# A hand-written order list of 1364 words, dealt anew behind its first 60 words

## The chip, the core and the metric

The kernel runs on one core of one Trainium2 chip. The metric is the device time of one execution in microseconds (us), lower is better. The engines that matter here are TensorE (PE, with its weight loads as a row of their own, PEld), VectorE (DVE), ScalarE (ACT), GpSimd (POOL) and SyncE (SP), which in this kernel does nothing but issue transfers.

## The reference

Two branches read the same layer-normalised input `xn` (2048 rows of 512) and are added to the input:

```python
x = A_x                                   # 1 x 2048 x 512, bf16
xn = _layernorm(x, axis=-1)
return x + _A_ref(xn, A_wq, A_wk, A_wv, A_wo, A_beta) + _B_ref(xn, B_w1, B_w2)
```

Branch B is `silu(xn @ w1) @ w2` with 1792 hidden columns. Branch A is attention with 32 heads of 16 in four segments of 512 rows. In each segment every head does causal softmax attention inside the segment (`a_dot`), and besides reads a memory of the earlier segments (`a_mem = phi(q) M / (phi(q) z)`, with `phi(t) = t + 1` above zero and `exp(t)` below); the two are mixed by a gate, `g * a_mem + (1 - g) * a_dot`, and the result goes through `wo`. After each segment `M` and `z` grow by the segment's keys and values.

## The kernel before, in words

**Tiles and banks.** Everything is kept in SBUF: the transposed `xnT`, all weights, and per segment the tiles `qT`, `kT`, `hT` (hidden activations) and `oT` (attention output). PSUM has eight banks. Four belong to `psS`, the scores of one step; the other four are a pool (`pb`) from which every other sum takes one bank: `ps` (projections, hidden sums, the memory product), `psV` (weights times values), `psM` and `psO` (an output row block). A sum that needs a bank waits until an earlier holder was copied out by DVE or ACT.

**The order list.** The program is not written as loops. A string `ORDER` holds 1364 words, and the last loop of the kernel calls one small function a word, in the order of the list. An engine runs its own instructions in exactly that order, so the list sets each engine's queue, and the words of different engines only stand beside each other. The words that the text needs, with segment `s` and column group or row block as numbers:

- `S0` to `S71`: a score step (`scores`, L716): TensorE multiplies queries by keys in four row strips into `psS`, ACT takes the exponential of all 2048 columns (L722, into one of six buffers `Pb`), POOL masks (L736). A line break in the list stands ahead of each `S`.
- `E0`, `O0` and so on: weights times values (`weigh`, L783), even and odd heads, in column strips; `Ev`, `Ov`, `Ea`, `Oa` copy the bank out (DVE or ACT) and move the softmax sums to the tile `zraw` by two small transfers (L805); `Om` merges odd heads into `oraw`.
- `h`, `ha`, `hv`: hidden sums, tanh on ACT (L483), and the product on DVE (L488). `k`, `q`, `v` with `kv`, `qv`, `vv`: projections and their copies.
- `r`, `w` (last segment: `R`, `W`): reciprocals of the sums (L536, L551) and the gate (L541, L557); `z`, `d` spread them over partitions by two transfers each (L568, tile `spr`), `zv`, `dv` multiply (L580, L590); `n`, `nv` are the memory product and its addition into `oT` (L599).
- `o`, `oc`, `od`: one output product (512, 256 or 128 columns) of a row block; each block needs 18 of the 512-column kind, 14 from `hT` and 4 from `oT`. `xl` loads the residual rows (L605), `st` adds them and stores the block (L612 on DVE, then the store's issue at L617). `oh` and `sh`: the last block is summed and stored in two halves (256 columns each, L659 and the store's issue at L663).

These last words, above all the `o` family, are filler: they may stand nearly anywhere behind their inputs, and they fill TensorE between the score steps.

**One piece or four strips.** A 128-column product is issued either as one matmul (L336) or as four matmuls of 32 columns side by side (L338). Which it is follows from the list: a product behind an `S` takes the form of the next `S`, `E`, `O` or like word, so that TensorE changes its tile form as seldom as can be. 

Of the kernel before, what the change touches and what calls it, by code (L numbers as in the profile page):

```python
# [19 lines left out]
S3 v0.2.0 v0.2.1 Nv4 h0.1.2 h0.1.3 v0.2.2 XD7 v0.2.3 K0.1 hv0.0 vv0.2 k0.2.1 k0.2.2 k0.2.3 kv0.2 XD4 ha0.1  # L20
S1 lw1.1 v0.3.0 tanh v0.3.1 fa0.1 omask h0.2.0 h0.2.1 lw0.12 xs8 q0.3.0 fp0.0 v0.3.2 lw0.13 lw0.5 v0.3.3 h0.2.2 q0.3.1
S4 q0.3.2 q0.3.3 Nv6 hv0.1 vv0.3 lw1.3 qv0.3 lw0.1 XD6 v1.3.0 v1.3.1 v1.3.2 xs11 h0.4.0 h0.2.3 ha0.2 v1.3.3 vv1.3 h0.3.0 XD5 hv0.2
S5 h0.4.1 K0.2 h0.3.1 h0.4.2 kind h0.3.2 h0.3.3 ha0.3 fv0.1 h0.4.3 E0
S6 v1.0.0 v1.0.1 v1.0.2 v1.0.3 Ev0 fp0.3 ha0.4 hv0.3 vv1.0 v1.2.0 v1.2.1 v1.2.2 xs10 v1.2.3 q1.0.0
S7 vv1.2 xs9 xg8.4 q1.0.1 q1.0.2 h0.6.0 h0.6.1 O0 hv0.4 Ov0 fa0.3 h0.6.2 lw0.10 h0.6.3
S8 q1.0.3 qv1.0 E1 Ev1 fv0.3 q1.1.0 q1.1.1 ha0.6 h0.8.0 h0.8.1 q1.1.2
S9 v1.1.0 hv0.6 Nv10 q1.1.3 Om0 v1.1.1 Nv11 qv1.1 v1.1.2 v1.1.3 k1.2.0 gp1.1 vv1.1 k1.2.1 t0.3 fa0.2 k1.2.2 k1.2.3
S12 fv0.0 kv1.2 K0.3 h0.8.2 h0.5.0 h0.5.1 h0.5.2 h0.5.3 XD11 ha0.5 fp0.2 Nv8 XD10 XD8 h0.7.0 h0.7.1 h0.7.2 hv0.5 h0.8.3 ha0.8 hv0.8
S10 q1.2.0 q1.2.1 q1.2.2 q1.2.3 qv1.2 h0.7.3 k1.0.0 lw0.9 t0.1 ha0.7 Nv9 lw1.2 k1.0.1 k1.0.2 XD9 k1.0.3 h0.10.0 kv1.0
S13 h0.10.1 O1 hv0.7 Ov1 q1.3.0 q1.3.1 q1.3.2 k1.3.0 q1.3.3 qv1.3 ga1.1  # L30
S11 fv0.2 h0.10.2 fp1.0 k1.3.1 t0.2 t0.0 k1.3.2 k1.3.3 xs15 kv1.3 h1.1.0 h1.1.1 h0.10.3 k1.1.0 lw0.0 lw0.11 ha0.10 h1.1.2 h1.1.3 ha1.1 hv0.10
S15 k1.1.1 hv1.1 h0.9.0 h0.9.1 h0.9.2 E2 K1.0 h0.9.3 ha0.9 h1.2.0 xs14 gv1.1 hv0.9 h1.2.1
S14 h1.2.2 h1.2.3 Ev2 k1.1.2 k1.1.3 kv1.1 xs12 ha1.2 hv1.2 O2 k2.2.0 lw0.4
S17 h1.10.0 h1.10.1 k2.2.1 kv2.2 lw1.0 h1.10.2 h1.10.3 ha1.10 gate h0.11.0 h0.11.1 h0.11.2 Ov2 lw0.8 lw0.6
S16 h0.12.0 h0.11.3 ha0.11 h0.12.1 h0.12.2 hv1.10 E3 Om2 Ev3 lw0.2 lw0.7 xl0.0 K1.1 hv0.11 k2.1.0 h0.12.3 ha0.12 K1.2
S20 k2.1.1 h0.13.0 h0.13.1 h0.13.2 kv2.1 hv0.12 O3 fp1.2 Ov3 m0.2 mv0.2 h0.13.3 fa1.0 Om1
S18 q2.1.0 q2.1.1 v2.2.0 m0.0 qv2.1 v2.2.1 lw0.3 ha0.13 fv1.0 K1.3
S19 mv0.0 k2.0.0 k2.0.1 hv0.13 v2.1.0 v2.1.1 kv2.0 fa1.2 h1.11.0
S22 vv2.2 sv0 r0.1 q2.3.0 vv2.1 h1.11.1 h1.11.2 xs13 xg12.4 o0.2.12 h1.11.3 q2.3.1 ha1.11 hv1.11 o0.2.7
S24 qv2.3 o0.2.4 od0.2.11.2 h1.8.0 h1.8.1 h1.8.2 h1.8.3 o0.2.13 h1.0.0 oc0.2.6.0 o0.2.1 od0.2.11.1 ha1.8 r0.2 r0.0  # L40
S25 E4 o0.2.2 h1.0.1 r0.3 w0 o0.2.8 z0.1 h1.0.2 h1.0.3 xl0.2 ha1.0 z0.2 hv1.8 Ev4 od0.2.11.0 h1.7.0 Nv15
S21 hv1.0 K2.1 h1.4.0 h1.7.1 h1.4.1 fv1.2 h1.7.2 h1.7.3 ha1.7 Nv12 XD12 hv1.7 q2.0.0 q2.0.1 XD15
S23 o0.2.3 qv2.0 h1.4.2 h1.4.3 ha1.4 o0.2.0 od0.2.11.3 fp1.1 z0.0 zv0.1 O4 z0.3 Ov4 k2.3.0
S26 zv0.2 fp1.3 k2.3.1 h1.9.0 h1.9.1 h1.9.2 h1.9.3 hv1.4 ha1.9 o0.0.8 K2.0 kv2.3 hv1.9 o0.0.5 o0.0.15
S31 E5 o0.0.4 bmask o0.0.2 od0.0.1.1 oc0.0.3.0 oc0.0.7.1 h1.13.0 Ev5 o0.0.10 fa1.3 h1.13.1
S28 Om3 O5 o0.0.6 Ov5 o0.0.13 Nv13 od0.0.1.0 o0.0.9 h1.13.2 h1.13.3 ha1.13 hv1.13 h1.3.0
S27 oc0.0.7.0 fv1.3 h1.3.1 oc0.0.3.1 h1.3.2 h1.3.3 xl0.3 od0.0.1.2 oc0.2.6.1 zv0.0 h1.12.0 ha1.3 h1.12.1 h1.12.2 hv1.3 XD13 gp1.2 t1.3 h1.12.3 ha1.12 hv1.12 Om5 oc0.2.10.1
# [5 lines left out]
S34 mw0.0 fv2.1 o0.3.7 h1.6.0 o0.3.10 h1.6.1 o0.3.8 od0.3.2.2 od0.3.2.0 Om4 h1.6.2 h1.6.3 oc0.1.2.1 o0.3.11 ha1.6 hv1.6 gp1.3
S40 mw0.2 ga1.3 K2.3 o0.1.1 o0.3.4 O7 Ov7 gv1.3 q3.1.0 q3.1.1 xl0.1 qv3.1 oc0.3.3.0
S42 k3.1.0 o0.1.10 o0.3.13 k3.1.1 kv3.1 oc0.3.1.0 od0.3.2.3 oc0.1.2.0 o0.3.5 m1.2 mv1.2
S36 o0.1.13 o0.1.4 ga2.2 st0.3 od0.1.8.2 s1 sv1 gp2.2 v2.3.0 o0.1.5 K2.2 xl1.1 o1.2.12 r1.0 o0.1.0 m1.0
S37 fp2.0 v2.3.1 o0.1.12 Om6 mv1.0 vv2.3 o0.1.6 o1.2.10 Om7 q3.3.0 fa2.0 q3.3.1
S38 r1.1 qv3.3 h2.8.0 h2.8.1 v3.3.0 t2.1 ha2.8 v3.3.1 r1.3 r1.2 w1 o1.2.8 z1.3
S39 st0.1 hv2.8 od1.2.0.0 od1.2.0.2 vv3.3 z1.1 q3.2.0 q3.2.1 E8 Ev8 v3.0.0 d1.3
S41 qv3.2 v3.0.1 h2.11.0 o1.2.1 d1.2 h2.11.1 k3.0.0 ha2.11 zv1.3  # L60
S49 vv3.0 h1.5.0 h1.5.1 fv2.0 t2.0 h1.5.2 h1.5.3 ha1.5 hv2.11 o1.2.3 gv2.2 k3.0.1 kv3.0 z1.2 E9 hv1.5
S44 fp2.2 k3.2.0 ga2.1 k3.2.1 o1.2.13 xl1.2 v3.2.0 v3.2.1 Ev9 kv3.2 dv1.3
S43 vv3.2 zv1.1 h2.7.0 n1.3 nv1.3 gp2.1 h2.7.1 ha2.7 zv1.2 q3.0.0 q3.0.1
S48 qv3.0 d1.1 d1.0 O8 Ov8 o1.2.6 dv1.2 h2.5.0 h2.5.1 ha2.5 hv2.7 o1.2.4 oc1.2.11.1
S45 oc1.2.2.1 z1.0 K3.2 O9 hv2.5 h2.1.0 Ov9 dv1.0 h2.1.1 dv1.1 ha2.1 h2.12.0
# [869 lines left out]
```

## Time and profile before

| | |
|---|---|
| time, median of 3 runs | 221.25 us (220.82, 221.25, 221.46) |
| the profiled execution's own time | 221.0 us |
| span of that execution, first to last instruction | 219.2 us |
| TensorE busy | 211.5 us (96%) |
| ACT busy | 184.2 us (84%) |
| DVE busy | 180.2 us (82%) |
| POOL busy | 126.7 us (58%) |
| granted TensorE clock | 0.999 |

The times of the profile are counted from the start of the span. Between the span and the execution's own time lie 1.8 us outside the program's instructions. A busy TensorE says only that a matmul was in the pipe; whether it waits is read from its waits and from the stretch in which they fall.

### The profile page before, as it was taken

Reading aid. Unit: us, or ns where it says so; the run is one execution under the profiler, and the core shown is the slowest. Engines: PE = TensorE matmul, PEld = TensorE weight load, DVE = VectorE, ACT = ScalarE, POOL = GpSimd, SP = SyncE. Lnnn points to the kernel's source line nnn. Section 1 sums busy time; section 2 is a strip of 40 time slices with the busy share of each in tenths; the row PEclk is TensorE's granted clock in tenths of the full one; section 3 lists DMA queues with packets and bytes.
Section 4 is the critical chain, followed back from the end, with each engine's and each line's share of the span. In section 5 each row is a group of like instructions: output and inputs, shape, how many; then the busy total and the mean of one; then the engine's idle time right before and its main releaser. Section 6 shows DMA issues by size and latency. Waiting matters only on the chain.

```text
span 219.2 us, 9430 instructions
## 1 busy us (share of the span) xinstructions
PE 211.5 (96%) x4058; PEld 116.5 (53%) x4084; DVE 180.2 (82%) x367; ACT 184.2 (84%) x175; POOL 126.7 (58%) x189
## 2 busy tenths in 40 slices
...
GB/s 199 361 372 126 169 28 52 121 87 114 125 28 13 91 74 73 51 99 7 98 52 82 90 63 15 24 11 98 74 54 89 88 52 82 65 4 88 110 52 99
DMA packets 33530, 19.62 MB, mean 90 GB/s; under 512 B 14928, under 2 KB 33488, under 8 KB 33488
## 3 DMA queue, kind: packets, MB, share of 16 engines
...
q8 instruction: 32, 0.52, 1.0%
...
## 4 chain that ended last, share of the span: by engine, by line
PE 85%; ACT 10%; DVE 2%; issue 1%
PE ps L336 19%; PE psO L338 17%; PE ps L338 16%; PE psS L716 10%; PE psO L336 9%; PE psV L783 8%; ACT Pb L722 6%; PE psS L338 4%; PE psS L856 2%; ACT th L483 1%; ACT ex L414 1%; PE psM L443 1%; ACT L309 1%; ACT xnT L843 0%; ACT Vz L397 0%
## 5 line engine op out<-in xcount | busy, mean ns | idle before, releaser
L722 ACT ACTIVATE Pb<-psS 128x2048 bf16<-128x2048 f32 x72 | 135.2, 1878 | 4.0 <-PE psS L716 2.7
L736 POOL TENSOR_SCALAR_AFFINE_SELECT Pb<-Pb 128x512 bf16<-128x512 bf16 (+1 forms) x72 | 60.0, 834 | 29.8 <-ACT Pb L722 27.0
L488 DVE SCALAR_TENSOR_TENSOR hT<-th,ps 128x512 bf16<-128x512 bf16 x56 | 37.5, 678 | 12.9 <-ACT th L483 12.3
L338 PE MATMUL psO<-w_sb,hT 128*32 128x512 bf16 (+2 forms) x712 | 43.5, 324 | 0.0
L736 POOL TENSOR_SCALAR_AFFINE_SELECT lows<-Pb 64x512 bf16<-64x512 bf16 (+1 forms) x40 | 23.6, 590 | 25.8 <-ACT Pb L722 18.1
L483 ACT ACTIVATE th<-ps 128x512 bf16<-128x512 f32 x56 | 32.6, 596 | 2.2 <-PE ps L338 1.6
L336 PE MATMUL ps<-xnT,w_sb 128*128 128x512 bf16 (+1 forms) x143 | 32.6, 336 | 0.5 <-issue 0.2
L338 PEld LDWEIGHTS <-hT 128*32 128x32 bf16 x880 | 22.2, 97 | 14.5 <-issue 2.3
L338 PE MATMUL ps<-xnT,w_sb 128*32 128x512 bf16 (+1 forms) x516 | 28.8, 337 | 0.0
L716 PE MATMUL psS<-qT,k 32*128 32x64 bf16 (+3 forms) x512 | 23.0, 233 | 0.3
L716 PEld LDWEIGHTS <-k 32*128 32x128 bf16 x512 | 9.7, 92 | 22.6 <-issue 21.8
L783 PE MATMUL psV<-Pb,Vz 128*32 128x448 bf16 (+7 forms) x512 | 21.4, 287 | 0.0
L336 PE MATMUL psO<-w_sb,hT 128*128 128x512 bf16 (+2 forms) x83 | 20.5, 319 | 0.6 <-issue 0.5
L783 PEld LDWEIGHTS <-Vz 128*32 128x32 bf16 x768 | 15.8, 97 | 9.2 <-issue 1.3
L336 PEld LDWEIGHTS <-w_sb 128*128 128x128 bf16 x151 | 13.6, 98 | 11.9 <-issue 2.3
L338 PEld LDWEIGHTS <-w_sb 128*32 128x32 bf16 x516 | 12.9, 97 | 7.4 <-issue 1.1
L382 POOL TENSOR_SCALAR k<-kT,pm_odd 128x512 bf16<-128x512 bf16 x16 | 11.6, 725 | 8.2 <-DVE stats L286 7.1
L716 PE MATMUL psS<-qT,kT 16*128 16x448 bf16 (+3 forms) x256 | 14.7, 269 | 0.0
L612 DVE SCALAR_TENSOR_TENSOR o_out<-psO,x_res 128x512 bf16<-128x512 f32 x14 | 9.6, 688 | 5.9 <-PE psO L338 2.7
L336 PE MATMUL ps<-wv_sb,xnT 128*128 128x512 bf16 x46 | 13.5, 385 | 1.0 <-ACT xnT L843 0.5
L336 PEld LDWEIGHTS <-hT 128*128 128x128 bf16 x88 | 8.2, 98 | 8.8 <-issue 1.3
L820 DVE CAST odd<-psV 128x512 bf16<-128x512 f32 x15 | 10.3, 687 | 3.0 <-PE psV L783 2.8
...
## 6 DMA issues: line engine op xcount, KB each, us to landing
...
```

What stands on the lines that cost most here:

```text
L336: return [nc.tensor.matmul(out, lhsT=lhsT, rhs=rhs, start=start, stop=stop, skip_group_check=True)]
L338: nc.tensor.matmul(out[c : c + 32], lhsT=lhsT[:, c : c + 32], rhs=rhs, start=start, stop=stop, tile_position=(0, c), skip_group_check=True,)
L382: nc.gpsimd.tensor_scalar(out=to, in0=frm, scalar1=keep[:, 0:1], scalar2=1.0, op0=ALU.mult, op1=ALU.mult)
L483: nc.scalar.activation(out=th[:], in_=sts[s]["h", ft][:, :], func=AF.Tanh, scale=0.5)
L488: nc.vector.scalar_tensor_tensor(out=st["hT"][:, ft, :], in0=st.pop(("th", ft))[:], scalar=1.0, in1=st.pop(("h", ft))[:, :], op0=ALU.add, ...
L612: out = nc.vector.scalar_tensor_tensor(out=o_out[:], in0=st.pop(("psO", j)), scalar=0.5, in1=st["x", j][:], op0=ALU.mult, op1=ALU.add)
L716: nc.tensor.matmul(psS[:, g, c : c + q2 - q1], lhsT=keys[rows], rhs=st["qT"][rows, dt, q1:q2], start=True, stop=True, tile_position=(32 * ...
L722: exp = nc.scalar.activation(out=blocks(Pb, b).rearrange("p x g c -> p g x c"), in_=psS[:, :, :].rearrange("p g (x c) -> p g x c", c=block ...
L736: over[id(Pb)].append(nc.gpsimd.affine_select(out=out, in_=in_, compare_op=ALU.is_ge, fill=0.0, base=base, pattern=pattern, channel_multip ...
L783: nc.tensor.matmul(psV[32 * g : 32 * g + 32, q0 : q0 + nq], lhsT=Vzs[s % 2][:, kt, 4 * dt + g, par : par + 2, :].rearrange("p a d -> p (a ...
L820: copy(out=odd[:], in_=sts[s].pop(("psV", 1))[:, :])
L856: nc.tensor.matmul(idle[:, 0:P], lhsT=zraw[:, 0:P], rhs=zraw[:, 0:P], start=True, stop=True)
```

## The change

The list behind its first 60 words is replaced by another list of the same 1364 words. Two of the shorter lines, before and after:

```diff
 ORDER = """
...
-S35 q2.2.0 q2.2.1 o0.1.3 qv2.2 o0.1.16 E7 Ev7 fa2.1 oc0.1.9.0
...
+S35 q2.2.0 q2.2.1 fa2.1 o0.1.14 Om5 o0.3.5 E7 oc0.1.2.0
...
```

The old list ends with the words `st3.1 oh17.1 o3.2.16 o3.0.6 od3.0.2.2 o3.2.17 st3.2 oh17.0 o3.0.17 o3.0.8 o3.0.11 st3.0 oh0.0 oh1.1 oh11.1 oh12.1 oh11.0 oh15.1 oh9.1 oh6.1 oh8.1 sh1 oh10.0 oh7.0 oh16.0 oh6.0 oh13.0 sh0`, the new one with `st3.2 oh17.1 oc3.0.1.1 st3.0 oh16.1 oh14.1 oh7.1 oh15.1 oh2.1 oh14.0 oh9.0 oh10.0 oh12.0 oh16.0 oh6.0 oh13.0 sh1 oh0.0 oh2.0 oh5.0 oh1.0 oh17.0 oh7.0 oh4.0 oh15.0 sh0`.

In the new list `O9` stands between `O8` and `Ov8`, so that two odd sums are open at once. The kernel therefore keeps them under a key with the column group:

```diff
-        psV = st["psV", par] = bank([P, L], F32, "psV")
+        psV = st["psV", par, dt] = bank([P, L], F32, "psV")
...
-        copy(out=oraw[:], in_=sts[s].pop(("psV", 0))[:, :])
+        copy(out=oraw[:], in_=sts[s].pop(("psV", 0, dt))[:, :])
...
-        copy(out=odd[:], in_=sts[s].pop(("psV", 1))[:, :])
+        copy(out=odd[:], in_=sts[s].pop(("psV", 1, dt))[:, :])
```

All words are the same, so every transfer, activation and vector operation is there as often as before. TensorE issues 4033 matmuls instead of 4084, since 17 products come in one piece instead of four strips.

Where the order moved, at two places that the prediction speaks of. First VectorE near the end of the program, from the reciprocals of the last softmax sums on. `RECIPROCAL ri<-zraw 32x64` are the last four reciprocals (L551), which wait for the sums of the last odd heads; `rz` is their gate (L557), `phiQT<-spr` and `oT<-spr` are products with spread sums, `o_out<-psO` is the copy-out of a finished output block, `oT<-ps` the addition of the memory product. Before:

```order
L551 RECIPROCAL ri<-zraw 32x64
L590 TENSOR_TENSOR phiQT<-spr,phiQT 128x512
L551 RECIPROCAL ri<-zraw 32x64
L590 TENSOR_TENSOR phiQT<-spr,phiQT 128x512
L551 RECIPROCAL ri<-zraw 32x64
L580 TENSOR_TENSOR oT<-spr,oraw 128x512
L551 RECIPROCAL ri<-zraw 32x64
L612 SCALAR_TENSOR_TENSOR o_out<-psO,x_res 128x512
L557 TENSOR_SCALAR rz<-ri,gate 32x256
L599 TENSOR_TENSOR oT<-ps,oT 128x512
```

and after:

```order
L488 SCALAR_TENSOR_TENSOR hT<-th,ps 128x512
L590 TENSOR_TENSOR phiQT<-spr,phiQT 128x512
L827 COPY_PREDICATED oraw<-omask,odd 128x256
L590 TENSOR_TENSOR phiQT<-spr,phiQT 128x512
L551 RECIPROCAL ri<-zraw 32x64 x4
L557 TENSOR_SCALAR rz<-ri,gate 32x256
L612 SCALAR_TENSOR_TENSOR o_out<-psO,x_res 128x512
L580 TENSOR_TENSOR oT<-spr,oraw 128x512 x2
L599 TENSOR_TENSOR oT<-ps,oT 128x512 x2
```

The four reciprocals now stand in a row, behind the last hidden product and two products that stood between them before, and the copy-out of the block stands behind their gate instead of ahead of it.

Second SyncE's queue over the last transfers: `zraw` are the moves of the softmax sums, `spr` the spreads, `x_res` residual loads, `out_dram` the stores. Before:

```order
L805 DMA zraw<-oraw 4x256 x2
L805 DMA zraw<-odd 4x256 x2
L568 DMA spr<-rz 128x1x256 x2
L605 DMA x_res<-in_A_x_dram 128x512 x2
L568 DMA spr<-rz 128x1x256 x4
L617 DMA out_dram<-o_out 128x512
L605 DMA x_res<-in_A_x_dram 128x512
L568 DMA spr<-rz 128x1x256 x2
L617 DMA out_dram<-o_out 128x512
L605 DMA x_res<-in_A_x_dram 128x512
L617 DMA out_dram<-o_out 128x512 x3
L663 DMA out_dram<-o_half 128x256 x2
```

and after:

```order
L605 DMA x_res<-in_A_x_dram 128x512
L805 DMA zraw<-oraw 4x256 x2
L805 DMA zraw<-odd 4x256 x2
L568 DMA spr<-rz 128x1x256 x6
L617 DMA out_dram<-o_out 128x512
L568 DMA spr<-rz 128x1x256 x2
L617 DMA out_dram<-o_out 128x512
L605 DMA x_res<-in_A_x_dram 128x512 x2
L617 DMA out_dram<-o_out 128x512 x3
L663 DMA out_dram<-o_half 128x256 x2
```

A residual load moved ahead of the last moves, the last spread stands behind a block's store now, and the last three block stores and the two half stores close the queue in both.

More of the change, by code (lines that the diff above doesn't have):

```diff
@@ L20 @@
[L20 to L47, printed above, removed]
@@ L53 @@
[L53 to L65, printed above, removed]
@@ new lines @@
+ones0 ones1 zeros xc0 busy41 xd0 xc1 xq0 xi0 xd1 xq1 Nv0 X0.1 xc2 Xa0.1 xi1 Nv1 v0.0.0 xd2 xq2 X1.1 Xa1.1 xs3 xq3 v0.0.1 v0.0.2 v0.0.3 va0.0 xi2 Nv2 v0.1.0 v0.1.1 v0.1.2 X2.1 xi3 tb Nv3 v0.1.3 odd X3.1 Xv2.1 k0.1.0 k0.1.1 Xv3.1 va0.1 k0.0.0 k0.0.1 k0.0.2 k0.0.3 ka0.0 K0.0 fa0.0 q0.0.0 q0.0.1 q0.1.0 q0.0.2 q0.0.3 q0.1.1 q0.1.2 q0.1.3 qa0.0 kind qa0.1 fp0.0
+S2 q0.2.0 k0.1.2 k0.1.3 ka0.1 k0.3.0 xs6 xs4 xs7 xs5 xg4.4 k0.3.1 k0.3.2 q0.2.1 q0.2.2 k0.3.3
+S0 q0.2.3 qv0.2 h0.0.0 h0.0.1 h0.0.2 h0.0.3 kv0.3 Nv7 ha0.0 hv0.0 h0.1.0 h0.1.1 Nv5 k0.2.0 fp0.1
@@ new lines @@
+S3 K0.1 v0.2.0 v0.2.1 XD7 v0.2.2 v0.2.3 vv0.2 h0.1.2 h0.1.3 h0.2.0 Nv6 ha0.1 hv0.1 k0.2.1 k0.2.2
+S1 lw0.7 v0.3.0 omask k0.2.3 h0.2.1 h0.2.2 kv0.2 fa0.1 v0.3.1 Nv4 v0.3.2 v0.3.3 vv0.3 q0.3.0 q0.3.1
+S4 xs8 h0.2.3 ha0.2 K0.2 q0.3.2 q0.3.3 qv0.3 fv0.1 h0.4.0 XD5 fp0.3 xs11 XD4 h0.4.1 v1.3.0 v1.3.1 v1.3.2 v1.3.3
+S5 h0.3.0 h0.4.2 h0.3.1 hv0.2 XD6 t0.1 h0.3.2 h0.3.3 ha0.3 h0.4.3 vv1.3 lw0.13 E0 Ev0
+S6 v1.0.0 v1.0.1 v1.0.2 v1.0.3 v1.2.0 v1.2.1 hv0.3 xs10 vv1.0 v1.2.2 v1.2.3 q1.0.0 ha0.4 hv0.4 xs9 xg8.4
@@ new lines @@
+S9 q1.0.1 q1.0.2 vv1.2 q1.0.3 qv1.0 O0 fa0.3 Ov0 h0.6.0 h0.6.1 h0.6.2
+S7 E1 q1.1.0 q1.1.1 q1.1.2 Ev1 h0.6.3 h0.8.0 ha0.6 lw1.0 h0.8.1 Nv9
+S11 v1.1.0 v1.1.1 v1.1.2 fv0.3 hv0.6 v1.1.3 lw0.3 Nv8 q1.1.3 k1.2.0 lw0.8 fa0.2 qv1.1 Nv11 XD9 k1.2.1 k1.2.2 k1.2.3 vv1.1
+S8 h0.5.0 h0.5.1 h0.5.2 h0.7.0 K0.3 Nv10 XD10 h0.5.3 Om0 h0.8.2 kv1.2 fv0.0 ha0.5 h0.8.3 ha0.8 XD11 h0.7.1 h0.7.2 fp0.2 t0.0
+S10 xl0.1 hv0.5 XD8 q1.2.0 q1.2.1 q1.2.2 q1.2.3 qv1.2 k1.0.0 k1.0.1 hv0.8 h0.7.3 ha0.7 k1.0.2 k1.0.3 kv1.0 q1.3.0
@@ new lines @@
+S16 h0.12.1 E3 Ev3 lw0.11 h0.12.2 h0.12.3 h0.13.0 K1.1 h0.13.1 Om2 ha0.12 hv0.12 h0.11.2 h0.11.3 ha0.11
+S20 k2.1.0 h0.13.2 lw0.4 h0.13.3 m0.2 hv0.11 k2.1.1 mv0.2 O3 lw0.12 kv2.1 Ov3 fa1.0
+S18 fv1.0 q2.1.0 lw0.10 q2.1.1 m0.0 mv0.0 fp1.3 qv2.1 ha0.13 v2.2.0 v2.2.1 vv2.2
+S22 tanh h1.11.0 k2.0.0 k2.0.1 v2.1.0 xs13 xg12.4 hv0.13 v2.1.1 fa1.2
+S19 sv0 h1.11.1 h1.11.2 kv2.0 q2.3.0 q2.3.1 o0.2.1 h1.11.3 o0.2.2 lw1.1 ha1.11
+S24 o0.2.13 od0.2.11.3 gate oc0.2.6.0 vv2.1 h1.8.0 r0.3 K2.0 qv2.3 h1.8.1 h1.8.2 h1.8.3 o0.2.12 h1.0.0 r0.0 o0.2.8 ha1.8 od0.2.11.1
@@ new lines @@
+S25 r0.1 hv1.11 r0.2 w0 lw1.2 z0.0 hv1.8 h1.7.0 h1.0.1 od0.2.11.0 t1.0 Om3 o0.2.0 h1.0.2 h1.0.3 E4 h1.7.1 z0.1 ha1.0
+S21 Ev4 z0.3 o0.2.7 h1.7.2 hv1.0 q2.0.0 bmask Nv15 h1.7.3 ha1.7 q2.0.1 qv2.0 h1.4.0 h1.4.1 z0.2
+S23 o0.2.4 O4 h1.4.2 h1.4.3 ha1.4 hv1.7 zv0.0 o0.2.3 Ov4 fv1.2 gp1.0 hv1.4 od0.2.11.2 k2.3.0
+S26 Nv12 XD12 h1.9.0 h1.9.1 k2.3.1 kv2.3 h1.9.2 h1.9.3 ha1.9 o0.0.11 XD15 o0.0.8 o0.0.10
+S31 zv0.1 o0.2.15 o0.0.15 E5 hv1.9 o0.2.9 Ev5 fa1.3 oc0.0.7.1 od0.0.1.1 h1.13.0 h1.13.1 zv0.2 oc0.0.3.0
@@ new lines @@
+S40 gp2.2 fv2.1 o0.1.4 r1.0 v2.3.1 vv2.3 o1.2.12 xl1.2 o0.1.13 st0.1 fa2.0 q3.3.0 r1.2 q3.3.1 r1.3
+S38 v3.3.0 v3.3.1 qv3.3 h2.8.0 K2.2 h2.8.1 w1 z1.3 o1.2.8 vv3.3 d1.3 ha2.8 hv2.8
+S39 q3.2.0 v3.0.0 od1.2.0.3 od1.2.0.2 z1.1 q3.2.1 Om7 E8 Ev8
+S41 qv3.2 v3.0.1 vv3.0 o1.2.1 zv1.3 h2.11.0 h2.11.1 k3.0.0 ha2.11 hv2.11 gv2.2
+S49 k3.0.1 kv3.0 h1.5.0 z1.2 h1.5.1 d1.2 fp2.0 o1.2.3 Om6 h1.5.2 h1.5.3 ha1.5 E9 Ev9
+S44 ga2.1 o1.2.13 v3.2.0 v3.2.1 dv1.3 hv1.5 od1.2.0.1 k3.2.0 k3.2.1 vv3.2 zv1.1 kv3.2
+S48 fv2.0 n1.3 h2.7.0 d1.0 h2.7.1 nv1.3 ha2.7 dv1.2 q3.0.0 q3.0.1 hv2.7 qv3.0
```

72 lines of the change are left out of this document (41 added, 31 removed).

## The prediction

> **What bounds the kernel now.** I read the page first, then who waited for whom on TensorE, then the busy time by stretch, then the last microseconds by time. From the page, busy time and the shares of the chain that ended last:
>
> ```profile
> PE 211.5 (96%) x4058; PEld 116.5 (53%) x4084; DVE 180.2 (82%) x367; ACT 184.2 (84%) x175; POOL 126.7 (58%) x189
> ...
> PE 85%; ACT 10%; DVE 2%; issue 1%
> ```
>
> TensorE is the bound, with ACT close by. The waits of TensorE, longest in total first, and the busy time of the engines by 10 us stretches (PE, PEld, DVE, ACT, POOL; then clock, DMA share, GB/s):
>
> ```profile
> PE psS L856 <- DVE zraw L185: 1.1, 1, 1.1
> ...
> PE ps L336 <- ACT xnT L843: 0.5, 1, 0.5
> ```
>
> ```profile
> 0.00:10.00 10.00, 8.38 (x72) 6.86 (x74) 7.30 (x22) 5.67 (x13) 3.49 (x15) 1.00 0.86 271
> 10.00:20.00 10.00, 9.76 (x110) 7.10 (x109) 7.54 (x16) 9.90 (x13) 5.03 (x9) 1.00 0.89 294
> ...
> 190.00:200.00 10.00, 10.00 (x256) 6.21 (x252) 7.71 (x16) 4.17 (x6) 0.73 (x1) 1.00 0.10 32
> 200.00:210.00 10.00, 10.00 (x260) 6.39 (x252) 7.42 (x15) 0.00 (x0) 0.00 (x0) 1.00 0.45 119
> 210.00:220.00 10.00, 5.52 (x148) 3.74 (x140) 3.61 (x6) 0.00 (x0) 0.00 (x0) 0.93 0.18 57
> sum 220.00, PE 211.48 PEld 116.48 DVE 180.17 ACT 184.23 POOL 126.65; mean PE 9.61 PEld 5.29 DVE 8.19 ACT 8.37 POOL 5.76
> ```
>
> No wait on another engine's work in the middle is long enough to be listed: the two that are (1.1 and 0.5 us) belong to the start, for the first zeros and the first transposed rows. The stretches say how much an order can win at all. From 20 to 210 us TensorE is busy 211.48 - 8.38 - 9.76 - 5.52 = 187.82 of 190 us, so 2.2 us are idle; the first 20 us lose 1.9. What is left at the end is 219.2 less the last matmul at 215.5, 3.6 us, which no matmul fills. In the middle the two engines run in step:
>
> ```profile
> 100.32 1.88 ACT L722 ACTIVATE Pb<-psS 128x2048 bf16<-128x2048 f32 x1
> 102.10 0.62 ACT L414 ACTIVATE ex<-qT 128x512 bf16<-128x512 bf16 x1
> 102.27 0.21 PE L716 MATMUL psS<-qT,k 32*128 32x64 bf16 x4
> 102.73 1.88 ACT L722 ACTIVATE Pb<-psS 128x2048 bf16<-128x2048 f32 x1
> ```
>
> An exponential ends at 102.20, the next score step, which needs its `psS`, starts at 102.27, and ACT fills the gap with one short activation before the next exponential 2.41 us after the last. TensorE's filler is measured to fit this beat, so a score step that comes early only waits, and one that comes late makes ACT idle.
>
> **The change part by part.** (1) TensorE's work. 17 products lose their strips. What a product costs in either form stands in the chain of waits, start, length, what:
>
> ```profile
> 135.52 0.86 PE ps L338 x16
> ...
> 140.66 0.86 PE ps L336 x4
> ```
>
> Sixteen strips are four products of 512 columns, 0.215 us each, and four whole ones take the same 0.215 us: 17 x 0 = 0. All other products are the same ones in another order, and the form of the array changes 144 times in both lists, in and out of each of the 72 score steps. Term: 0, within 0.1 us.
>
> (2) The beat. On ACT both lists show a step's exponential followed by the same number and kinds of short activations in nearly every gap; only some three places, the gate's tanh, steps 54 to 57 and the last two steps, differ by one. Summing the products between score steps at 0.215 us a 512-column one, each of the first 69 steps stands within 0.4 us of its old place. Term: 0. The idle 2.2 us bound a gain here; a loss is bounded below under the rivals. I take -0.1 us, since most of the old steps already start within 0.1 us of the exponential's end, as above.
>
> (3) The head. The first 60 words are untouched, and the 1.9 us of idle TensorE in the first 20 us stand with them: 0.
>
> (4) The end. Here the profile shows something that can move. The last rows by time, and the issues of the two half stores by themselves (duration in ns, shortest/median/longest):
>
> ```profile
> 215.02 0.97 DVE L659 SCALAR_TENSOR_TENSOR o_half<-psS,x_res 128x256 bf16<-128x256 f32 x2 [0.29 <-PE psS L338]
> 215.47 1.57 SPq L663 DMA_DIRECT2D out_dram<-o_half  x2
> ```
>
> ```profile
> L663 SPq DMA_DIRECT2D out_dram<-o_half x2: 383/736/1090, 215.5 to 216.7; - x2
> ```
>
> The last half is copied at 215.02 + 0.97 = 215.99, but its store is issued at 216.66, because the first half's issue took 1.09 us instead of 0.38. Without that the last store would go out 0.03 us after its copy (as the first did: 215.44 to 215.47), at 216.02: **0.64 us** of the end are this one late issue. Is it luck? Issues by kind:
>
> ```profile
> L617 SPq DMA_DIRECT2D out_dram<-o_out x15: 333/347/1340, 90.9 to 214.8; - x15
> L605 SPq DMA_DIRECT2D x_res<-in_A_x_dram x16: 376/443/1257, 58.6 to 208.3; - x16
> L432 SPq DMA_TRANSPOSE phiK<-pk x12: 1188/1216/2474, 35.2 to 152.4; - x12
> L568 SPq DMA_DIRECT2D spr<-rz x56: 602/632/711, 69.5 to 205.2; - x56
> L805 SPq DMA_DIRECT2D zraw<-odd x32: 496/515/562, 32.4 to 197.0; - x32
> ```
>
> Stores, residual loads and transposes are long now and then, by 0.7 to 1.3 us; spreads and moves never. The page's queues, and the DMA view of three stretches, each with one long issue (the half store at 215.47, a residual load at 199.45, a store at 166.51):
>
> ```profile
> q8 instruction: 32, 0.52, 1.0%
> ```
>
> ```profile
> q8 instruction: 1, 0.02, 5.6%
> ```
>
> ```profile
> q8 instruction: 1, 0.02, 4.2%
> ```
>
> ```profile
> q8 instruction: 1, 0.02, 4.3%
> ```
>
> Each of the three overlaps one of the 32 packets of the instruction queue. The packets are 0.52 MB / 32 = 16 KB, and TensorE alone has 4084 loads and as many matmuls, 8168 / 32 = 255 a packet: they are fetches of TensorE's program, and each comes at a fixed place of it. The 32nd comes at 215.2, when only about four of the 8168 are left, so it hits the half store in every run. The new program has 102 fewer (2 x 51). The fetch 256 places earlier then falls 256 - 102 + 4 = 158 places before the end: twenty half-width products of eight (four loads, four matmuls), and a 32nd does not come. In the new list twenty half-width products stand behind the store of block 0 and eight, not five, behind the first half. Their price is in the chain of waits:
>
> ```profile
> 213.99 1.55 PE psS L338 x56
> ```
>
> 14 products in 1.55 us, 0.11 us each. So the last fetch starts 2.2 us before the last matmul and is over when the first half's store is issued (0.9 us of products, less 0.45 for the copy, so 0.4 before). It may meet the store of block 2; a long issue there would be 1.0 us of which the queue behind it gives back all but 0.3. And if the first half's issue is long all the same, it starts 3 x 0.11 = 0.33 us earlier and the last store gains 0.33. Term: between -0.33 and -0.64; I take **-0.64**, as nothing is seen to meet it.
>
> The Trainium skill speaks of these fetches ("Runtime: NRT & Kernel Launch", section Instruction fetch mechanics): the program is refilled in blocks of 16 KiB, 256 instructions, over the sequencer's own DMA queue, and the cost of a block boundary is mostly hidden. The 32 packets agree with the size; by "mostly hidden" alone term (4) would be nothing and the sum 221.2, while the 1.09 us issue here says otherwise.
>
> (5) The last sums. VectorE's rows before, with the move of the last odd sums on SyncE ahead of them:
>
> ```profile
> 196.41 1.06 SPq L805 DMA_DIRECT2D zraw<-odd  x2
> ```
>
> ```profile
> 198.63 0.55 DVE L551 RECIPROCAL ri<-zraw 32x64 f32<-32x64 bf16 x1 [0.69 <-DMA zraw<-odd]
> ...
> 202.56 0.69 DVE L612 SCALAR_TENSOR_TENSOR o_out<-psO,x_res 128x512 bf16<-128x512 f32 x1 [0.33 <-DMA x_res<-in_A_x_dram]
> 203.28 0.35 DVE L557 TENSOR_SCALAR rz<-ri,gate 32x256 bf16<-32x256 f32 x1
> ```
>
> Placed by the products that stand ahead of each word, the new order runs so: the last hidden product comes at about 198.2 (its matmuls end at 197.5, the tanh takes 0.6), then three short ones at a third of a us, four reciprocals at 0.56 and the gate at 0.35: 0.6 + 1.0 + 2.2 + 0.35 = 4.2, so VectorE is free at 202.4, just as block 1 of segment 2 is summed (202.5 by the products ahead of it, 202.7 with the pipe). Its copy ends at 203.4. TensorE's first memory product needs that bank and stands at 203.6: no wait, with 0.2 us in hand. Against that, the old wait for a residual load (0.33) goes, since the load is issued some 7 us earlier, and the reciprocals no longer wait for the sums. Term: 0, and up to +1.7 below.
>
> Sum, against the profiled execution: 221.0 - 0.64 - 0.1 = 220.3. The median of the runs shown, 221.25, is 0.25 above that execution; on its footing the change gives 220.5, and with a tenth for a wait somewhere among 1300 moved words **220.6**.
>
> **The rivals.** *The late store comes again* (or came by chance): then only the -0.1 is left and the time is 221.2. For it speaks that not each fetch hits an issue that is long; against it the three rows above.
>
> *More is won*: the small waits of the middle, 2.2 us of idle TensorE at most, are halved as well: 220.6 - 1.1 = 219.5. Against it speaks the beat: steps start 0.07 us after an exponential's end already, and ACT has no less to do.
>
> *Slower*: the first memory product waits. TensorE takes its words in order, so all behind it wait too, and the last spread stands in SyncE's queue behind this block's store. It decides from the moment when VectorE gets to the copy later than 202.7. The train of nine ahead of it has 0.2 us in hand at its own durations, and the sums' landing, 1.7 us after its issue before, has about 1.5. One long issue in front (0.7 to 1.3) is absorbed; a landing or a tanh later than that passes on in full, and with two long issues (0.7 + 1.3) and the 0.2 the loss is about 1.7: 220.6 + 1.7 = 222.3.
>
> *It does not do what it says*: the orders differ everywhere, so this one is only that nothing happens, which is the first rival's 221.2.
>
> **How the numbers follow.** No change can be told from less than 0.3%, 0.66 us: below 220.6 is faster, above 221.9 slower. My forecast has 0.55, its own range 220.1 to 221.0, and sits on the edge, so three fifths of it, 0.33, count as faster and 0.22 as the same. The late store again has 0.22 (same). More won has 0.09 (faster), slower 0.14. Faster 0.42, same 0.44, slower 0.14. The range reaches from 219.9, the forecast's lower end with a little of the second rival, to 221.8, which takes in the first rival and the lighter half of the slow one.
>
> **What would show it.** Right: 31 fetches; the two half stores' issues both near 0.4 us and the last store some 0.03 us behind its copy; the last matmul at 215.4 within 0.3; TensorE busy about 211.5. The beat would be right if most score steps still start within 0.1 us of an exponential's end. Wrong: a row of TensorE waiting for the copy-out (L612) or for a spread near 203 to 210 (then the slow rival), or a half store's issue of 1 us again. If the last matmul comes over 1 us later than 215.5 with TensorE idle in the middle, the list has lost the beat and term (2) is the step that failed.

## The result, and the profile after

| | before | after |
|---|---|---|
| time, median of 18 runs each | 221.22 us (220.72 to 222.68) | 219.95 us (219.46 to 220.76) |
| ratio | | 0.9946, 95% interval 0.9931 to 0.996 |
| the profiled execution's own time | 221.0 us | 220.76 us |
| its span | 219.2 us | 219.0 us |

The new list is 0.54% faster, 1.27 us. The profiled execution of the kernel after is the slowest of its 18, so its span must be read with care: it holds a wait that the other four profiles of this list (runs 2, 5, 8 and 12 below) do not have. The page's lines, then the waits of TensorE, then the instruction queue:

```profile
PE 213.4 (97%) x4033; PEld 117.1 (53%) x4033; DVE 176.4 (81%) x367; ACT 184.4 (84%) x175; POOL 125.2 (57%) x189
...
PE 78%; ACT 9%; SPq 4%; issue 3%; DMA 3%; DVE 1%; DVEq 0%
```

```profile
PE psS L856 <- DVE zraw L185: 1.1, 1, 1.1
PE ps L338 <- DVE oT L599: 0.7, 1, 0.7
PE ps L336 <- ACT xnT L843: 0.5, 1, 0.5
```

```profile
q8 instruction: 31, 0.51, 1.0%
```

There are 31 fetches instead of 32, and a new wait of 0.7 us for `oT`. The end of the program, first the issues of the two half stores (duration in ns, shortest, median, longest), then VectorE's and SyncE's last rows:

```profile
L663 SPq DMA_DIRECT2D out_dram<-o_half x2: 332/332/332, 215.7 to 216.5; - x2
```

```profile
215.22 0.42 DVE L659 SCALAR_TENSOR_TENSOR o_half<-psS,x_res 128x256 bf16<-128x256 f32 x1 [0.24 <-PE psS L338]
216.10 0.42 DVE L659 SCALAR_TENSOR_TENSOR o_half<-psS,x_res 128x256 bf16<-128x256 f32 x1 [0.45 <-PE psS L338]
```

```profile
215.67 1.21 SPq L663 DMA_DIRECT2D out_dram<-o_half  x2
```

Both issues are short now, and the last store goes out at 216.55, 0.03 us behind its copy (216.52). Before, it went out 0.67 us behind it. The place where the new wait comes from, on SyncE, VectorE and TensorE:

```profile
196.75 3.97 SPq L568 DMA_DIRECT2D spr<-rz  x6
```

```profile
202.38 0.69 DVE L612 SCALAR_TENSOR_TENSOR o_out<-psO,x_res 128x512 bf16<-128x512 f32 x1 [0.42 <-PE psO L338]
...
204.27 0.42 DVE L580 TENSOR_TENSOR oT<-spr,oraw 128x512 bf16<-128x512 bf16 x1 [0.87 <-DMA spr<-rz]
204.61 0.68 DVE L599 TENSOR_TENSOR oT<-ps,oT 128x512 bf16<-128x512 f32 x1
```

```profile
205.35 0.40 PE L338 MATMUL ps<-phiQT,Mbf 128*32 128x512 bf16 x4 [0.74 <-DVE oT L599]
```

The copy-out (L612), of which the prediction was afraid, waits only for TensorE's own product. But the last of the six spreads in a row lands 0.87 us late; its product (zv3.1) stands ahead of the copy of the first memory product (nv3.0), whose bank the second memory product needs.

To compare the lists without such single waits, three numbers are read from the timeline of each profile: the start of the first exponential (S), the time from it to the start of the last matmul (W, TensorE's work with its waits), and from there to the end of the span (E). For the kernel before, the kernel after, and the undisturbed fifth run below the rows are

```profile
12.94 1.88 ACT L722 ACTIVATE Pb<-psS 128x2048 bf16<-128x2048 f32 x1
...
215.12 0.40 PE L338 MATMUL psS<-w_sb,hT 128*32 128x256 bf16 x8
```

```profile
12.76 1.88 ACT L722 ACTIVATE Pb<-psS 128x2048 bf16<-128x2048 f32 x1
...
215.75 0.30 PE L338 MATMUL psS<-wo_sb,oT 128*32 128x256 bf16 x4
```

```profile
12.83 1.88 ACT L722 ACTIVATE Pb<-psS 128x2048 bf16<-128x2048 f32 x1
...
214.91 0.28 PE L338 MATMUL psS<-wo_sb,oT 128*32 128x256 bf16 x4
```

where the last matmul of the row starts at 215.25, 215.78 and 214.92, and the spans end at 219.19, 219.04 and 218.17. All profiles of this study, read in the same way (the last column is the start of a fetch of TensorE's program behind 213):

| kernel | S | W | E | fetch at the end |
|---|---|---|---|---|
| before | 12.94 | 202.31 | 3.94 | 215.21 |
| run 1, before, program 24 shorter | 12.47 | 202.56 | 4.20 | 215.08 |
| run 9, before, load earlier | 13.30 | 202.33 | 3.99 | 215.14 |
| run 10, before, transpose earlier | 13.05 | 202.67 | 3.65 | 215.21 |
| run 6, before, program 36 shorter | 12.77 | 202.72 | 3.39 | 219.25 |
| run 11, before, all three | 12.56 | 202.64 | 5.26 | 217.27 |
| run 7, before, program 204 longer | 13.01 | 204.25 | 3.26 | none |
| run 4, after, then the tail of before | 13.14 | 202.41 | 3.26 | 219.41 |
| after | 12.76 | 203.02 | 3.26 | none |
| run 5, after, program 24 shorter | 12.83 | 202.09 | 3.25 | none |
| run 8, after, one product later | 12.89 | 202.09 | 3.25 | none |
| run 12, after, load later | 12.82 | 202.09 | 3.27 | none |
| run 2, after, program 102 longer | 12.81 | 202.18 | 3.67 | 214.92 |

(Run 3 is left out; its cut made a wait of its own.) Three things stand in it. E is 3.95 on average in the four profiles of the old list with a fetch at 215.1 to 215.2, and 3.26 in the four of the new list without one: **0.69 us**. W is 202.31 at its least with the old list and 202.09 with the new: **0.22 us** of TensorE's time. And W is disturbed in four of the six profiles with the old list (runs 7 and 4 aside) by 0.25 to 0.4 us, and in one of five with the new one, by 0.93: the medians are 202.60 and 202.09, **0.51 us**. S varies from 12.47 to 13.30 with the same first 60 words, and not with the list (means 12.87 for the seven rows of the old list, 12.88 for the six that begin with the new one). The two medians together, 0.69 + 0.51 = 1.20, come near the 1.27 measured; the undisturbed parts alone, 0.69 + 0.22 = 0.91, lie at the interval's edge (0.4% of 221.22 is 0.88).

Runs 5, 7 and 9 each had one execution in a slow state of the chip (421.7, 224.92 and 227.16 us), which the medians and ratios below leave out.

### The profile page after: what moved, and what is told of

Read it like the earlier page. It is cut to its first block, busy times and chain, and to the rows that moved or that the text cites. A ratio compares the mean times of both kernels' runs of the same rounds, so it can differ in the third digit from the quotient of the medians.

```text
span 219.0 us, 9350 instructions
## 1 busy us (share of the span) xinstructions
PE 213.4 (97%) x4033; PEld 117.1 (53%) x4033; DVE 176.4 (81%) x367; ACT 184.4 (84%) x175; POOL 125.2 (57%) x189
## 4 chain that ended last, share of the span: by engine, by line
PE 78%; ACT 9%; SPq 4%; issue 3%; DMA 3%; DVE 1%; DVEq 0%
PE ps L336 20%; PE ps L338 14%; PE psO L338 13%; PE psS L716 10%; PE psO L336 9%; PE psV L783 7%; ACT Pb L722 5%; DMA spr<-rz 3%; PE psS L338 2%; PE psS L856 2%; SPq L568 2%; ACT th L483 2%; SPq L805 1%; ACT ex L414 1%; PE psM L443 1%
## 5 line engine op out<-in xcount | busy, mean ns | idle before, releaser
L736 POOL TENSOR_SCALAR_AFFINE_SELECT Pb<-Pb 128x512 bf16<-128x512 bf16 (+1 forms) x72 | 61.1, 849 | 26.2 <-ACT Pb L722 23.3
L488 DVE SCALAR_TENSOR_TENSOR hT<-th,ps 128x512 bf16<-128x512 bf16 x56 | 37.8, 681 | 17.5 <-ACT th L483 16.7
L338 PE MATMUL psO<-w_sb,hT 128*32 128x512 bf16 (+2 forms) x672 | 40.8, 324 | 0.0
L336 PE MATMUL ps<-xnT,w_sb 128*128 128x512 bf16 (+1 forms) x162 | 35.4, 340 | 0.0
L338 PE MATMUL ps<-xnT,w_sb 128*32 128x512 bf16 (+1 forms) x472 | 26.6, 333 | 0.0
L336 PE MATMUL psO<-w_sb,hT 128*128 128x512 bf16 (+2 forms) x98 | 23.7, 323 | 0.0
L336 PEld LDWEIGHTS <-w_sb 128*128 128x128 bf16 x162 | 14.9, 98 | 11.8 <-issue 1.5
L338 PEld LDWEIGHTS <-w_sb 128*32 128x32 bf16 x472 | 11.5, 97 | 6.2 <-issue 1.6
L336 PEld LDWEIGHTS <-hT 128*128 128x128 bf16 x98 | 9.0, 98 | 10.6 <-issue 2.4
L338 PE MATMUL psO<-wo_sb,oT 128*32 128x512 bf16 x152 | 14.2, 380 | 0.0
L612 DVE SCALAR_TENSOR_TENSOR o_out<-psO,x_res 128x512 bf16<-128x512 f32 x14 | 9.5, 682 | 3.8 <-PE psO L338 3.7
```

The costliest lines, as they stand in the source:

```text
L336: return [nc.tensor.matmul(out, lhsT=lhsT, rhs=rhs, start=start, stop=stop, skip_group_check=True)]
L338: nc.tensor.matmul(out[c : c + 32], lhsT=lhsT[:, c : c + 32], rhs=rhs, start=start, stop=stop, tile_position=(0, c), skip_group_check=True,)
L488: nc.vector.scalar_tensor_tensor(out=st["hT"][:, ft, :], in0=st.pop(("th", ft))[:], scalar=1.0, in1=st.pop(("h", ft))[:, :], op0=ALU.add, ...
L612: out = nc.vector.scalar_tensor_tensor(out=o_out[:], in0=st.pop(("psO", j)), scalar=0.5, in1=st["x", j][:], op0=ALU.mult, op1=ALU.add)
L736: over[id(Pb)].append(nc.gpsimd.affine_select(out=out, in_=in_, compare_op=ALU.is_ge, fill=0.0, base=base, pattern=pattern, channel_multip ...
```

## The experiments

The kernel before had 221.1 to 221.25 us beside all of these. The ratios given with their 95% intervals differ by up to 0.25% from the quotient of the two medians (run 12 most). Theory F: the last store of the kernel before is late because the 32nd fetch of TensorE's program overlaps the first half store's issue.

**Run 1: the old list, the program 24 instructions shorter.**

```diff
-        for i in range(n):
-            nc.tensor.matmul(idle[:, 0:P], lhsT=zraw[:, 0:P], rhs=zraw[:, 0:P], start=True, stop=True)
+        for i in range(n - 12):
+            w = 2 * P if i < 12 else P
+            nc.tensor.matmul(idle[:, 0:w], lhsT=zraw[:, 0:P], rhs=zraw[:, 0:w], start=True, stop=True)
```

> The list before, word for word; of the 41 warm-up products at the start 12 take 256 columns and 12 fall away, so the columns are the same and TensorE's program is 24 instructions shorter (8144 loads and matmuls instead of 8168). Theory F (the long issue of the first half store is the 32nd fetch of TensorE's program): 31 packets of the instruction queue, both half stores issued in about 0.38 us, the time 0.64 us below the kernel before, about 220.6. Rival (the long issue has another cause): an issue of about 1.1 us stays, or the time stays at 221.2 within 0.2.

Measured: 221.75 us, ratio 1.0029 (1.0007 to 1.0051). The edit was too small: the fetch still came, at 215.08, and the half store's issue was long again:

```profile
L663 SPq DMA_DIRECT2D out_dram<-o_half x2: 383/866/1348, 215.3 to 216.7; - x2
```

So 24 instructions did not move the last fetch off the end. Nothing on F follows from the time; the half us it lost is taken up at run 5.

**Run 2: the new list with 18 products in strips again, and three warm-up products fewer, so that the program is as long as before.** The part of the edit that makes the strips:

```diff
+    strips = [(words.index(a), words.index(b)) for a, b in (("S22", "S19"), ("S41", "S49"))]
...
             now = "whole" if now == "rows" else now
+            now = "cols" if any(a < i < b for a, b in strips) else now
```

> The list after, with 18 of its products (those between the score steps 22 and 19 and between 41 and 49) issued as four strips again and three warm-up products less, so that TensorE has 8168 loads and matmuls as before. Theory F: a 32nd packet near 215, the first half store's issue about 1.1 us, the last store some 0.6 us behind its copy, and the time 0.33 to 0.64 us above the kernel after: 220.3 to 220.6. Rival (another cause; strips cost nothing): 219.95 within 0.2.

Measured: 220.9 us, ratio 0.9991 (0.9973 to 1.0009), so 0.95 us over the kernel after: with a program as long as before, three quarters of the gain are gone. The 32nd fetch came at 214.92. But it began 0.03 us after the first half store's issue, and that one stayed short:

```profile
L663 SPq DMA_DIRECT2D out_dram<-o_half x2: 332/404/475, 214.9 to 215.8; - x2
```

Only the second was lengthened, by 0.14, and from its start to the end of the span passed 2.9 us instead of the 2.5 to 2.6 of all other profiles but one (run 11). E is 3.67 against 3.26, W 202.18 against 202.09: the profile holds 0.50 of the 0.95 us; where the rest lies in the other executions is not shown. F holds as to the cause, a fetch at the end; the long issue is only one of the ways in which it costs.

**Runs 6 and 7: the old list without that fetch.** Run 6 is run 1 with 18 in place of 12. Run 7 leaves the warm-up alone and has strips in two early gaps:

```diff
+    strips = [(words.index(a), words.index(b)) for a, b in (('S2', 'S0'), ('S0', 'S3'))]
...
+            now = "cols" if any(a < i < b for a, b in strips) else now
```

> The list before with the warm-up cut by 18 products (8132 loads and matmuls, as many as the run in which no fetch came near the last matmul). Against the run with 12 products less, whose other fetches stand only 12 instructions apart from these. Theory F: no fetch near 215, two half stores of about 0.4 us, from the last matmul to the end of the span 3.25 us instead of 3.95, and a median 0.6 to 0.7 us below the 221.75 of that run, 221.1. Rival (the last store's delay is hidden by what follows it): 221.75 within 0.2.

> The list before, word for word, with the 17 products' worth of words between the score steps 2, 0 and 3 issued in four strips (102 more loads and 102 more matmuls than before, 8372), the warm-up untouched. The 32nd fetch then falls 208 instructions, some 2.9 us, ahead of the last matmul, near 212. Theory F: the half stores are 0.4 us each, last matmul to end 3.25 us, and 0.6 to 0.7 us less than before, 220.5, if the fetches' new places hit nothing else. Theory L: these places change the rest of the time by up to 0.6 us either way. Rival to F: 221.2.

Measured: 221.53 us, ratio 1.0022 (0.9995 to 1.0049), and 222.14 us, ratio 1.0046 (1.0026 to 1.0067). In both profiles no fetch meets the half stores and both issues are short, first run 6, then run 7:

```profile
L663 SPq DMA_DIRECT2D out_dram<-o_half x2: 332/332/332, 215.7 to 216.3; - x2
```

```profile
L663 SPq DMA_DIRECT2D out_dram<-o_half x2: 332/332/333, 217.5 to 218.0; - x2
```

E falls from 3.95 to 3.39 and 3.26: 0.56 and 0.69 us, about as F said. Yet the medians did not fall. In run 6 the eighth score step came 0.4 us late, its exponential waiting:

```profile
29.91 1.88 ACT L722 ACTIVATE Pb<-psS 128x2048 bf16<-128x2048 f32 x1 [0.41 <-PE psS L716]
```

Run 7 lost 0.35 us at the same step; TensorE stood still for 0.6 us among the strips at 16.7 to 17.3, with nothing named as the cause; and near the end a residual load landed so late that TensorE waited for the copy-out behind it (its waits, then VectorE's and TensorE's rows):

```profile
PE ps L338 <- issue: 0.6, 1, 0.6
```

```profile
204.96 0.69 DVE L612 SCALAR_TENSOR_TENSOR o_out<-psO,x_res 128x512 bf16<-128x512 f32 x1 [1.47 <-DMA x_res<-in_A_x_dram]
```

```profile
205.70 0.40 PE L338 MATMUL ps<-phiQT,Mbf 128*32 128x512 bf16 x4 [0.57 <-DVE o_out L612]
```

So F's 0.7 us is shown at the end of the profiles, and not in a median of the old list. For run 6 there is a second possible reason beside the late steps: the fetch has not gone, it comes at 219.25, and in run 11, with a program of the same length, it met the last store's landing. Where it fell in the other executions of run 6 is not known.

**Run 5: do the other fetches matter?** The new list with the cut of run 1.

> The list after with the same cut of the warm-up as in the first of the earlier four (12 products of 256 columns, 12 fewer), so that every fetch of TensorE's program falls 24 instructions later and everything else stays. Theory L (where the fetches fall among SyncE's issues makes a good part of the difference between the kernels; that run of the list before was 0.6 us over the list before itself): the median moves by 0.4 us or more, to 220.3 or above, and the profile has other issues lengthened, and more than the four of the kernel after. Rival (the list itself holds the gain, and the cut costs nothing): 219.95 within 0.2.

Measured: 219.78 us, ratio 0.9938 (0.9909 to 0.9966). The same as the kernel after: theory L falls for the new list. All fetches moved by 24 instructions and nothing changed. With the old list the same cut cost half a us in run 1, of which its profile shows 0.24 at the eighth score step and 0.26 in E. The new list does not mind where its fetches fall; the old one seems to.

**Runs 3 and 4: in which part of the list the gain lies.** Each takes one list as far as score step 62 and the other behind it; the few words that stand on different sides are put at the seam (`xl2.0 d2.1 dv2.3` in run 3, `xl2.2 d2.2` in run 4). Run 4 also has the warm-up cut of run 1, so 8132 loads and matmuls.

```diff
 run 3: -S62 h3.12.0 o1.1.9 o1.1.13 h3.7.0 dv2.0 st1.1 h3.7.1 ...
        +S62 h3.12.0 o1.1.9 o1.1.13 h3.7.0 dv2.0 st1.1 h3.7.1 xl2.0 d2.1 dv2.3 h3.12.1 z2.3 o2.0.1 ...
```

> The list before as far as score step 62 (1021 words), then the remaining words in the order of the list after; 8078 loads and matmuls, so no 32nd fetch by theory F. The measured gain is 1.27 us, of which F gives 0.64. If the other 0.6 lies in the last 40 us (theory T): 219.95, as the kernel after. If it lies ahead of step 62 (theory M, the beat or the head): 220.6.

> The list after as far as score step 62 (1022 words), then the remaining words in the order of the list before; the warm-up shortened as in the first of these four, so 8132 loads and matmuls and no 32nd fetch by theory F. Theory T (the other 0.6 us lies in the last 40 us): 220.6. Theory M (it lies ahead of step 62): 219.95.

Run 3: 223.85 us, ratio 1.0133 (1.0097 to 1.0168). It says nothing on the question, because my seam made a wait: VectorE comes to `dv2.3` when the spread that it needs has only just been issued, waits for the landing, and TensorE waits behind it:

```profile
165.72 0.42 DVE L590 TENSOR_TENSOR phiQT<-spr,phiQT 128x512 bf16<-128x512 bf16 x1 [1.72 <-DMA spr<-rz]
```

```profile
166.80 0.73 PE L783 MATMUL psV<-Pb,Vz 128*32 128x512 bf16 x16 [1.63 <-DVE hT L488]
```

Run 4: 221.06 us, ratio 1.0 (0.9978 to 1.0021), above both theories and nearer to T. Its profile divides W. The first exponential behind the seam, in the kernel before and in run 4, stands at

```profile
165.75 1.87 ACT L722 ACTIVATE Pb<-psS 128x2048 bf16<-128x2048 f32 x1
```

```profile
165.81 1.90 ACT L722 ACTIVATE Pb<-psS 128x2048 bf16<-128x2048 f32 x1
```

less S (12.94 and 13.14) that is 152.81 and 152.67: the new list gains 0.14 us as far as there. Behind it run 4 loses 0.24 (202.41 - 152.67 = 49.74 against 49.50), because with the old tail the residual load lands late, and the first memory product, whose bank this copy-out sets free, starts at 203.99 instead of 203.69:

```profile
203.24 0.69 DVE L612 SCALAR_TENSOR_TENSOR o_out<-psO,x_res 128x512 bf16<-128x512 f32 x1 [1.02 <-DMA x_res<-in_A_x_dram]
```

This led to theory R below.

**Run 8: the wait of the profiled execution after.**

```diff
-zv3.1 od3.0.2.0 n3.0 o3.2.9 o3.0.11 od3.0.2.2 o2.3.7 oc3.1.11.0 z3.3 nv3.0
+od3.0.2.0 n3.0 o3.2.9 o3.0.11 od3.0.2.2 o2.3.7 oc3.1.11.0 z3.3 nv3.0 zv3.1
```

> The list after with one word moved: the product with the last spread of block 1 (zv3.1) stands behind the copy of the first memory product (nv3.0) instead of ahead of it, so that a late landing of the sixth spread in the row no longer holds the bank that TensorE waits for. Theory W (this wait, 0.7 us on TensorE in the profiled execution of the kernel after, is taken by a part of its runs): the highest runs fall from 220.76 to about 220.1 and the median by 0.1 to 0.3, to 219.75. Rival (the wait comes only by chance in that one run, or the wait moves on to the second memory product): 219.95 within 0.1.

Measured: 220.06 us (219.28 to 220.40), ratio 0.9951 (0.9934 to 0.9968). The highest run is lower, the median is not: theory W falls. The order did change as meant (VectorE, the copy now ahead of the second product):

```profile
203.70 0.69 DVE L599 TENSOR_TENSOR oT<-ps,oT 128x512 bf16<-128x512 f32 x1 [0.17 <-PE ps L338]
204.31 0.41 DVE L580 TENSOR_TENSOR oT<-spr,oraw 128x512 bf16<-128x512 bf16 x1
```

but in runs 5, 12 and 2, which kept the old order of these words, no such wait appeared either (W 202.09, 202.09 and 202.18). The 0.93 us of the profiled execution were a late landing that none of these four profiles has.

**Runs 9 to 12: two suspected waits of the old list, one by one, together, and put back.**

```diff
 run 9 (before):  -... oh4.1 xl2.1 dv3.0 ...        +S71 hv3.10 xl2.1 R0.0 E15 ...
 run 10 (before): -... lw1.3 qv0.3 lw0.1 XD6 ... XD5 hv0.2    +... qv0.3 XD6 ... XD5 lw1.3 lw0.1 hv0.2
 run 11 (before): both, and the warm-up of run 6
 run 12 (after):  -... xl2.1 o2.1.3 ... R0.0 ...    +... z3.0 o3.2.7 o2.1.5 z3.2 xl2.1 ...
```

> The list before with one word moved: the residual load of block 1 of segment 2 (xl2.1) is issued ahead of the last moves of the softmax sums, some 4 us earlier, as the list after has it. Theory R (its landing is late by a varying amount, VectorE waits 0.3 to 1.5 us at that block's copy-out in the five profiles with this tail, and TensorE stands behind it when it is over 0.8): no wait of the copy-out for the load, the last matmul 25.2 us after the last exponential's start in the profile, the highest runs fall and the median goes 0.2 to 0.5 us below before, to 220.7 to 221.0. Rival (the wait has room everywhere but in one run): 221.15 within 0.15.

> The list before with two weight loads (lw1.3, lw0.1) moved behind the fourth transfer-transpose of the second quarter of the rows, so that the third one, which the eighth score step's gap waits for, is issued about 1 us earlier. Theory D (its landing is just in time in the profile of before, and 0.24 to 0.39 late in three of the other runs with this head): the eighth step never starts over 2.40 us behind the seventh, and the median falls by 0.1 to 0.3, to 220.85 to 221.05. Rival (the kernel before itself is not late there): 221.15 within 0.15.

> The list before with both moved words of the last two runs and the warm-up cut by 18 products, so that no fetch meets the half store. If the account F + R + D is whole, this is the kernel after within the 0.2 us of TensorE's work: no late store (3.25 us from the last matmul to the end), no wait for the residual load, the eighth step on time: 220.0 to 220.2. Rival (something else of the new list carries part of the gain): 220.5 or above.

> The list after with one word moved the other way: xl2.1 behind the first four of the six spreads, some 4 us later. Theory R: the copy-out of block 1 waits for its load again, here with the gate behind nothing of it but the memory product's bank, so that TensorE waits too: the median rises by 0.3 to 0.8, to 220.3 to 220.8. Rival: 219.95 within 0.15.

Measured: 221.07 us (ratio 1.0009, 0.9986 to 1.0031), 221.18 us (1.002, 1.0005 to 1.0035), 221.18 us (1.0001, 0.9981 to 1.0022) and 219.93 us (0.9965, 0.9952 to 0.9978). None of the expected moves came; run 10 is by its ratio even 0.2% slower than the kernel before. Run 9 has the wait for the load removed (VectorE's copy-out now waits for TensorE alone):

```profile
202.83 0.69 DVE L612 SCALAR_TENSOR_TENSOR o_out<-psO,x_res 128x512 bf16<-128x512 f32 x1 [0.22 <-PE psO L338]
```

and the median did not fall, so theory R falls: as long as the load is under some 0.7 us late, the wait is covered. Run 12, the reverse in the new list, agrees: loaded 4 us later, the row still waits for TensorE alone. It has five executions only, and its ratio shows a smaller gain than the kernel after's 0.9946 (the intervals overlap), so a small cost in the median is not excluded.

```profile
202.43 0.69 DVE L612 SCALAR_TENSOR_TENSOR o_out<-psO,x_res 128x512 bf16<-128x512 f32 x1 [0.42 <-PE psO L338]
```

Run 10 was on time at the eighth step, as run 9 was without the move, and lost 0.34 us elsewhere (ACT):

```profile
132.18 1.88 ACT L722 ACTIVATE Pb<-psS 128x2048 bf16<-128x2048 f32 x1 [0.41 <-PE psS L716]
```

So D explains single executions and not the median. Run 11 shows why the three together did not give the kernel after. Its half stores' issues are both short, but the last fetch had only moved to 217.27 to 218.15, into the landing of the last store, and the span ends 4.5 us behind that store's issue (215.97) instead of 2.5. The trace's packets show how: all of the store's are done by 217.15 but 18, about a sixteenth; the first of these starts at 218.13, as the fetch ends, and the last is done at 218.89. The queues in the stretch from 216.0 to 219.5, then the page's first line:

```profile
q8 instruction: 1, 0.02, 1.6%
```

```profile
span 220.5 us, 9419 instructions
```

In runs 4 and 6, with the same number of TensorE's instructions, this fetch came at 219.4 and 219.25, after the span; so at this length its place varies from one execution to the next. No kernel here beats the new list by more than can be measured (run 5: 219.78, run 12: 219.93).

## Why the prediction was right, and where it was off

219.95 us lies in the predicted range (219.9 to 221.8), at its lower end, 0.65 us below the 220.6 forecast: faster, where the forecast stood on the edge between faster and no change. The step that carries half of the gain was right; that the time lies inside the range all the same is in part luck, since the range reached down to 219.9 only for a little of the second rival, whose reason does not hold (below). By its steps:

1. *TensorE's work, 0 for the strips.* Right: run 2 gave 18 products their strips back and W grew by 0.09 us, 0.005 us a product.
2. *The beat, -0.1.* The step that was mis-sized: -0.22 us where neither list is disturbed, -0.51 between the medians of the profiles. 0.14 of the 0.22 lies ahead of the seam of run 4. The prediction looked only at waits in one profiled execution, and that one (W 202.31) was the best of the old list; four of the other five (runs 7 and 4 aside) lose 0.25 to 0.4 us at one step, the eighth in runs 1 and 6, another in runs 10 and 11, which the new list mostly does not. One such place was tried by itself (run 10) and is not the cause of the median; which places together make up the 0.29 us, and why the new list is spared them, is open. The sign that the prediction gave for the beat came: 44 of 71 score steps start within 0.1 us of an exponential's end, before 45.
3. *The head, 0.* Right: the means of S are 12.87 and 12.88, while single profiles lie up to 0.83 us apart.
4. *The late half store, -0.64.* Right in its cause and size: 31 fetches, both issues 332 ns, the last store 0.03 us behind its copy, E 0.69 us less. The place was counted a little wrong. The last fetch came 3.3 us ahead of the last matmul in the profile after, not 2.2. A program 24 shorter still has the 32nd at the last matmul (run 1, 8144 loads and matmuls), where by the count it should have gone; with 8132 it comes 2 to 4 us behind the last matmul (runs 11, 6 and 4), and with the 8066 of the new list not at all. On this fetch the Trainium skill ("Runtime: NRT & Kernel Launch", section Instruction fetch mechanics) says that a block boundary's cost is mostly hidden. The traces agree for the 31 of the new list, as far as run 5 tells (all moved, nothing lost), and disagree for the one at the end: 0.69 us in E, 0.95 us in the median of run 2.
5. *VectorE's last sums, 0 with up to +1.7.* Right: the copy-out waited only for TensorE. The rows that the prediction took for the slow rival did fire once, in the profiled execution itself, by way of the spread's landing: 0.7 us of TensorE, and a last matmul at 215.78 instead of 215.4 within 0.3. The undisturbed runs have it at 214.9 to 215.0, below that band, since step 2 gave more.

The rivals: the late store did not come again in the new list, and run 2 shows what it would have been, 220.9. "More is won" has the right sign and about half its size for a wrong reason. Its price came from 2.2 us of idle TensorE in the middle. The page before has 4058 matmuls for 4084 loads, so 26 have no record, and the idle rows that it names "issue" are of one product's length each:

```profile
PE ps L336 <- issue: 0.8, 5, 0.2
PE psO L336 <- issue: 0.5, 3, 0.2
```

After, all 4033 are recorded. Busy time from 20 to 190 us, before, then after, then run 9, the old list with one word moved, whose 4084 matmuls are all recorded:

```profile
20.00:190.00 170.00, 167.82 (x3243) 86.17 (x3267) 146.57 (x294) 164.49 (x146) 117.40 (x165) 1.00 0.29 70
```

```profile
20.00:190.00 170.00, 169.89 (x3224) 87.08 (x3222) 144.08 (x290) 164.89 (x146) 115.10 (x164) 1.00 0.27 70
```

```profile
20.00:190.00 170.00, 169.91 (x3272) 86.16 (x3271) 147.06 (x295) 164.48 (x146) 117.72 (x165) 1.00 0.30 70
```

TensorE seems 2.1 us busier after than before, but it is as busy with the old list when no record is missing. Most of that idle time was never there to be won. The sign "TensorE busy about 211.5" failed for the same reason (213.4).
